# First MLP of a fused attention and two-MLP kernel: three places where weight conversions stand in the engines' queues

## The chip, the cores and the metric

The kernel runs as one launch on one core of a Trainium2 chip. The metric is the device time of the launch in microseconds (us). Engines are named as in the profile: PE does matmuls (PEld loads their weights), DVE is the vector engine, ACT the scalar engine, POOL is GpSimd, and SP issues the DMAs of this kernel. Each engine works through its own queue in order; semaphores tie the queues together.

## What is computed

Clustered attention (2 batches, 8 heads, 768 tokens, head size 64; a query sees only the keys that fall to the same of 16 centroids), then two MLPs over the 1536 tokens of 512 features. The change lies in the first MLP.

```
x = attention output, 1536 x 512
h = x @ w_in                          # 512 -> 2048
x = (h / (1 + exp(-h))) @ w_out       # 2048 -> 512
gate = 1 / (1 + exp(-(x @ w_gate)))   # second MLP, 512 -> 1536
out = (gate * (x @ w_val)) @ w_out2   # 1536 -> 512
```

The weights come as 64-bit floats and are converted on the chip; every product is made of three matmuls on a high and a low half of each operand, so that float32 accuracy is kept.

## The kernel before

**Pairs.** The hidden features of the first MLP are worked on in eight pairs of 128-wide blocks, i = 0 to 7. A pair has two layers: `hidden(i)` makes the hidden features (PE names h_0x, h_0y, h_0z, h_0w, h_0v, h_1.. in the trace all read h_0), and `mixed(i)` multiplies them with the output weights (PE name y_) and adds them into `acc`. The hidden layer is one level of a Strassen scheme (`strassen`): seven runs of 12 matmuls, x, y, z, w, X, v, W, each on one PSUM bank, whose results DVE combines (L836, L838, L855, L846, L852). ACT applies the activation (L892) and casts the high half (L64, gha); DVE, for one quarter POOL, subtracts it for the low half (L869, gla): that is `split`, and `parted` holds the last one traced. PE's order is written by hand: for i from 2 on, the runs x and y of pair i come first, then `mixed(i - 1)`, then the other runs of pair i.

**Weights.** Each pair has two input blocks (ci) and two output blocks (co), with i and e or n as numbers. One block takes these steps: SP issues a 512 KB transfer into one of two raw buffers (ri, ro; L690); ACT copies the upper words into one of three buffers (L695); POOL clips (L696); DVE does three integer steps (L701, L703, L705); then ACT casts the high half (L64) and POOL subtracts for the low half (L714) of wi.. or wo... For an input block POOL makes four sums first (L741 to L744, si). The raw buffer is free for the next transfer when L705 is done. ACT's, DVE's and POOL's queues are put in order by a scheduler; `tc.issue_after(x)` lets an instruction stand only behind x in its engine's queue.

**What sets the place of the conversions.** `weights(key)` makes the block asked for and the next two. The list `behind` holds instructions of the attention's last head, behind which the first blocks' DVE steps are put one by one: nine row maxima, and three times an entry of `copied`, the DVE copies (L67) of transposed probabilities of the last head. `copied[-2]` is the copy of rows 2 and 3 of its second half (u7_1_2), `copied[-1]` that of rows 4 and 5 (u7_1_4).

**End of the attention.** PE makes the last value products v (L501) and the row sums' reciprocals spread over partitions, rb (L580); DVE adds and scales (L513, L574, L576, L587). Then ACT (L64) and DVE (L76) split two quarters of the second batch's operand x, and DVE's L836 frees the bank that h_0v of pair 0 needs.

Of the kernel before, what the change touches and what calls it, by code (L numbers as in the profile page):

```python
# [10 lines left out]
F32 = mybir.dt.float32  # L11
# [3 lines left out]
AF = mybir.ActivationFunctionType  # L15
# [16 lines left out]
def clustered_attention_then_two_mlps(ctx, tc, qT, kT, v, cen, cenT, w1i, w1o, w2g, w2v, w2o, out):  # L32
    nc = tc.nc
    B, HP, _, S = qT.shape
# [4 lines left out]
    NT = S // P  # L39
# [4 lines left out]
    scale = 1.0 / float(D) ** 0.5  # L44
    NPAIR = B * HP
# [10 lines left out]
    ends = []  # L56
    begin = []
    maxima = []
    copied, latest, moved = [], [], []
    home = {0: xp}  # L60

    def cast(eng, o, i):
# [22 lines left out]
    def right_sums(temporary, name, b, caster, adder, kept):  # L85

        put = partial(right_operand, name, b, caster=caster, subber=adder)
        b11, b21, b12, b22 = quarters(b).values()
        t1 = temporary(f"{name}t1{b}")
        adder.tensor_tensor(t1, b12, b11, op=ALU.subtract)  # L90
        kept[b] = t1
        t2 = temporary(f"{name}t2{b}")
        adder.tensor_tensor(t2, b22, t1, op=ALU.subtract)
        put("t2", t2)
        yield
        t4 = temporary(f"{name}t4{b}")
        adder.tensor_tensor(t4, t2, b21, op=ALU.subtract)
        put("t4", t4)
        yield
        t3 = temporary(f"{name}t3{b}")  # L100
        adder.tensor_tensor(t3, b22, b12, op=ALU.subtract)
        put("t3", t3)
        yield
# [577 lines left out]

    N1, N2 = M1 // 2, M2 // 2

    behind = [maxima[(NPAIR - 1) * 2 * NT + n] for n in (4, 7, 10) for _ in range(3)] + copied[-2:-1] * 3

    def converted(src, name):

        r = rp.tile([P, KD * P], mybir.dt.int64, tag="r", name=f"r{name}")
        with tc.issue_after(loaded[0].ins):
            nc.sync.dma_start(r, src)  # L690
        words = r.bitcast(I32).rearrange("p (n w) -> p n w", w=2)
        low, up_ = words[:, :, 0], words[:, :, 1]
        t = wp.tile([P, KD * P], F32, tag="c", name=f"c{name}")
        ti = t.bitcast(I32)
        nc.scalar.activation(t, up_.bitcast(F32), AF.Copy, scale=2.0**-112)  # L695
        nc.gpsimd.tensor_scalar(t, t, LARGEST, -LARGEST, op0=ALU.min, op1=ALU.max)  # L696
        def one():
            return tc.issue_after(behind.pop(0).ins) if behind else nullcontext()

        with one():  # L700
            nc.vector.tensor_scalar(ti, ti, 3, None, op0=ALU.logical_shift_left)  # L701
        with one():
            nc.vector.scalar_tensor_tensor(ti, low, 29, ti, op0=ALU.logical_shift_right, op1=ALU.bitwise_or)  # L703
        with one():
            nc.vector.scalar_tensor_tensor(ti, up_, SIGN, ti, op0=ALU.bitwise_and, op1=ALU.bitwise_or)  # L705
        return t
# [10 lines left out]
    def plain(src, name, after=()):  # L717
        return two(converted(src, name), name, after=after)

    def four(srcs, name):  # L720

        made = {}
        for n, src in enumerate(srcs):
            pair = two(converted(src, f"{name}_{n}"), f"{name}{n}")
            for m in range(2):
                made[f"a{n + 1}{m + 1}"] = part(pair, m)
        return made
# [6 lines left out]
    def seven(srcs, name, all_four=False):  # L734

        a, b = (converted(src, f"{name}_{n}") for n, src in enumerate(srcs))
        a11, a12, a21, a22 = a[:, 0:Q], a[:, Q:], b[:, 0:Q], b[:, Q:]
        first = two(a, f"{name}a")
        t = wp.tile([P, 4, Q], F32, tag="s", name=f"s{name}", bufs=1)
        sub = nc.gpsimd.tensor_tensor  # L740
        sub(t[:, 0], a21, a22, op=ALU.add)  # L741
        sub(t[:, 1], t[:, 0], a11, op=ALU.subtract)
        sub(t[:, 2], a11, a21, op=ALU.subtract)
        sub(t[:, 3], a12, t[:, 1], op=ALU.subtract)  # L744
        after = latest if all_four else ()
        s12 = two(t[:, 0:2].rearrange("p a b -> p (a b)"), f"{name}s", after=after)
        s34 = two(t[:, 2:4].rearrange("p a b -> p (a b)"), f"{name}t", after=after)
        last = two(b, f"{name}b") if all_four else two(a22, f"{name}d", dp)
        made = dict(
            a11=part(first, 0),  # L750
            a12=part(first, 1),
            s1=part(s12, 0),
            s2=part(s12, 1),
            s3=part(s34, 0),
            s4=part(s34, 1),
            a22=part(last, 1 if all_four else 0),
        )
        if all_four:
            made["a21"] = part(last, 0)
        return made  # L760

    jobs, place = [], {}
# [22 lines left out]
    def weights(*key):  # L785

        n = place[key]
        for c in range(n, min(n + look[0] + 1, len(jobs))):
            if c not in made:
                with tc.issue_after((ends if c > AHEAD else begin)[0].ins):  # L790
                    made[c] = jobs[c]()
        return made[n]
# [67 lines left out]
    parted = []  # L860
# [28 lines left out]
    def hidden(i, bs, order="xyzwXvW"):  # L889
        def take(c, m, h, bs, inside):  # L890
            g = c if inside else temporary(f"g{i}_{m}{h}{bs.start}")[:, bs]
            nc.scalar.activation(g, c, AF.Silu)  # L892
            split(g, m, (h, bs), f"a{i}", nc.gpsimd if m and h else nc.vector)

        yield from strassen(weights("1i", i), f"h{i}", take, bs, order)

    def hidden_directly(i, b):
        def take(c, m, b):
            g = temporary(f"g{i}_{m}_{b}")
            nc.scalar.activation(g, c, AF.Silu)  # L900
            split(g, m, (slice(0, 2), b), f"a{i}", nc.vector)

        yield from direct(weights("1i", i), f"p{i}", take, b)

    def accumulate(z, o, first):
        if first:
            nc.scalar.activation(z, o, AF.Copy)
        else:
            nc.vector.tensor_tensor(z, o, z, op=ALU.add)  # L909

    def mixed(i, b=None):
        f = [[gs[f"a{i}", k, t] for t in "hl"] for k in range(2)]
        if b is None:
            f = [[t.rearrange("p h b s -> p (h b s)") for t in k] for k in f]
            parts = [slice(n * NB, (n + 1) * NB) for n in range(B * S // NB)]
            z = acc.rearrange("p d h b s -> p d (h b s)")
        else:
            f = [[t[:, :, b, :] for t in k] for k in f]
            parts = range(2)
            z = acc[:, :, :, b, :]  # L920
        for n, c in enumerate(parts):
            for e in range(2):
                o = bank(f"y{i}_{n}{e}{b}", third(2 * n + e, b is not None))
                wh, wl = (h.rearrange("p (d k c) -> p d k c", d=2, k=2) for h in weights("1o", i, e))
                width = NB if b is None else HS
                for d in range(2):
                    for k, (fh, fl) in enumerate(f):
                        for m, (s, t) in enumerate(((wh, fh), (wh, fl), (wl, fh))):
                            nc.tensor.matmul(  # L929
                                o[:, d, 0:width],  # L930
                                lhsT=s[:, d, k, :],
                                rhs=t[:, c],
                                start=k == 0 and m == 0,
                                stop=k == 1 and m == 2,
                            )
                accumulate(z[:, 2 * e : 2 * e + 2, c], o[:, :, 0:width], i == 0)
                yield
# [36 lines left out]
    def out_of(i):  # L974
# [22 lines left out]
        def last_products(n, t, u):  # L997
            z = oc[:, t : u + 1 : u - t]
            h = NB // 2
            for m, (a, c) in enumerate(((0, slice(0, NB)), (1, slice(0, h)), (1, slice(h, NB)))):  # L1000
                o = bank(f"z{i}_{t}_{m}", third(n + m, True))
                for k in range(2):
                    products(o, t, u, k, (a,), c)
                accumulate(z[:, a, c], o[:, a, c], False)
                store((t, u)[a], z[:, a, c], c)

        def evict(o, t, u):
            z = oc[:, t : u + 1 : u - t]
            accumulate(z, o, i == 0)
            if i == N2 - 1:  # L1010
                for a, q in enumerate((t, u)):
                    store(q, z[:, a])
# [32 lines left out]
    def run(gen):  # L1045
        for _ in gen:
            pass
# [9 lines left out]
    def sums(name, b):  # L1057
        return right_sums(temporary, name, b, ACT, DVE, kept)
# [19 lines left out]
    next(following)  # L1078
    run(front)
    run(following)  # L1080
    rest = sums("x", 1)
    next(rest)
    with tc.issue_after(parted[0].ins):
# [86 lines left out]
```

## Time and profile before

| what | us |
|---|---|
| three runs, median (lowest to highest) | 785.38 (781.26 to 786.43) |
| the profiled execution, own time | 783.95 |
| its span in the trace | 782.0 |
| PE busy in it | 766.4 |

The span runs from the first to the last instruction of the program; 1.95 us of the profiled execution's own time lie around it. The profiled execution is 1.43 us below the median of the three runs.

### The profile page before, as it was taken

The numbers are of one execution on the slowest core, as the hardware profiler recorded it, in microseconds if no ns is written. First come the engines' busy times: TensorE is split into PE (matmuls) and PEld (weight loads), VectorE is DVE, ScalarE is ACT, GpSimd is POOL, SyncE is SP. The second block draws the span as 40 slices with busy tenths as digits, with TensorE's granted clock in tenths as the row PEclk, the third lists the DMA queues.
The fourth block names the chain that finished last, engine by engine and source line by source line (L and its number), as shares of the span: only waits on it lengthen the run. The fifth ranks groups of instructions, "written<-read, shape, count | busy, mean of one in ns | idle before, by whom it ended". The sixth has DMA issues, their size and how long they took to land.

```text
span 782.0 us, 11463 instructions
## 1 busy us (share of the span) xinstructions
PE 766.4 (98%) x4314; PEld 653.0 (83%) x4314; DVE 628.7 (80%) x787; ACT 404.6 (52%) x691; POOL 396.5 (51%) x345
## 2 busy tenths in 40 slices
PE   8999999999999998999999999999999999999998
PEld 4766776676768986989989989998998989999896
DVE  6887787788797988879688678998497896979746
ACT  6777776777786663615525326546532425333120
POOL 5234223646664774646546326445664847748220
PEclk9999999999999999999999999999999999999999
DMA  7676467368131132222121211221021221122004
GB/s 209 161 183 151 119 159 185 103 149 228 39 102 56 53 108 81 81 81 81 54 81 55 79 56 54 81 66 64 34 81 54 81 82 54 54 66 69 1 0 162
DMA packets 25487, 71.60 MB, mean 92 GB/s; under 512 B 4484, under 2 KB 4952, under 8 KB 25432
## 3 DMA queue, kind: packets, MB, share of 16 engines
q1 hardware_dynamic: 24888, 70.84, 31.1%
q8 instruction: 34, 0.56, 0.3%
q14 instruction: 21, 0.17, 0.1%
q10 hardware_dynamic: 544, 0.03, 0.0%
HBM read 48.01 MB, written 3.19 MB: 65 GB/s over the span
## 4 chain that ended last, share of the span: by engine, by line
PE 82%; DVE 9%; ACT 3%; DMA 3%; issue 2%; SPq 0%; POOL 0%; ACTq 0%; DVEq 0%; POOLq 0%
PE z L988 12%; PE v L501 7%; PE s L454 7%; PE y L929 4%; PE t L493 4%; PE h_0w L813 3%; PE h_0x L813 3%; PE g_0w L813 2%; PE g_0x L813 2%; PE y_00None L929 2%; PE u L482 2%; PE v_0w L813 2%; PE v_0x L813 2%; PE r L879 2%; PE q L879 2%; PE y_01None L929 2%
## 5 line engine op out<-in xcount | busy, mean ns | idle before, releaser
L462 DVE TENSOR_REDUCE nm<-s 128x1 f32<-128x768 f32 x96 | 91.5, 954 | 16.1 <-PE s L454 15.2
L467 ACT ACTIVATE e<-s,nm 128x768 f32<-128x768 f32 x96 | 86.5, 901 | 27.6 <-DVE nm L462 26.8
L988 PE MATMUL z<-wu,ghb 128*128 128x512 f32 (+1 forms) x292 | 89.7, 389 | 0.5 <-DVE acc L909 0.5
L501 PE MATMUL v<-ph,vv 128*64 128x384 f32 x384 | 69.2, 494 | 0.3 <-DVE ph L67 0.3
L988 PEld LDWEIGHTS z<-wu,ghb 128*128 128x128 f32 x292 | 54.0, 188 | 12.6 <-issue 1.3
L493 PE MATMUL t<-ident,e 128*128 128x128 f32 x384 | 58.7, 276 | 1.2 <-ACT ph L64 0.4
L454 PE MATMUL s<-ka,qa 128*128 128x384 f32 x192 | 57.5, 380 | 2.0 <-ACT e L467 1.7
L988 PE MATMUL z<-wu,glb 128*128 128x512 f32 (+1 forms) x146 | 57.1, 391 | 0.0
L532 POOL TENSOR_TENSOR acc<-xf,rb 128x768 f32<-128x768 f32 x7 | 12.8, 1829 | 83.8 <-DMA rb<-d_rb 83.8
L501 PEld LDWEIGHTS v<-ph,vv 128*64 128x64 f32 x384 | 25.2, 136 | 30.7 <-issue 26.2
L64 ACT ACTIVATE ph<-t 128x512 f32<-128x512 f32 x68 | 40.7, 599 | 17.9 <-PE t L493 17.0
L454 PE MATMUL s<-k,q 128*128 128x384 f32 x192 | 49.6, 339 | 0.1
L493 PEld LDWEIGHTS t<-ident,e 128*128 128x128 f32 x384 | 43.8, 140 | 5.7 <-DVE ph L67 3.2
L909 DVE TENSOR_TENSOR acc<-z,acc 128x1024 f32<-128x1024 f32 (+2 forms) x32 | 36.6, 1154 | 13.6 <-PE z L988 12.9
L482 PEld LDWEIGHTS u<-ident,e 128*128 128x128 f32 x192 | 22.8, 140 | 25.0 <-issue 18.6
L67 DVE COPY ph<-u 128x512 f32<-128x512 f32 x48 | 32.8, 683 | 12.4 <-PE u L482 12.4
L482 PE MATMUL u<-ident,e 128*128 128x128 f32 x192 | 38.8, 284 | 0.0
L454 PEld LDWEIGHTS s<-k,q 128*128 128x128 f32 x192 | 34.5, 188 | 0.6 <-DMA k<-rows 0.4
L988 PEld LDWEIGHTS z<-wu,glb 128*128 128x128 f32 x146 | 27.4, 188 | 7.3 <-DVE glb L869 1.8
L714 POOL TENSOR_TENSOR wo<-co,wo 128x512 fp32r<-128x512 f32 x16 | 23.1, 1449 | 20.3 <-ACT wo L64 20.3
L929 PE MATMUL y<-gha,wo 128*128 128x384 f32 x128 | 32.8, 334 | 0.0
L454 PEld LDWEIGHTS s<-ka,qa 128*128 128x128 f32 x192 | 28.9, 190 | 4.5 <-ACT e L467 3.4
(627 smaller groups left out, 2138.4 us busy)
## 6 DMA issues: line engine op xcount, KB each, us to landing
ri<-in_w1i SPq DMA_DIRECT2D x16, 512.0 KB, 3.2
ro<-in_w1o SPq DMA_DIRECT2D x16, 512.0 KB, 3.2
ka<-kh SPq DMA_DIRECT2D x32, 192.0 KB, 4.0
rg<-in_w2g SPq DMA_DIRECT2D x12, 512.0 KB, 3.2
rv<-in_w2v SPq DMA_DIRECT2D x12, 512.0 KB, 3.2
ru<-in_w2o SPq DMA_DIRECT2D x12, 512.0 KB, 3.4
qq<-in_qT SPq DMA_DIRECT2D x8, 384.0 KB, 3.3
kk<-in_kT SPq DMA_DIRECT2D x8, 384.0 KB, 5.0
```

The costliest lines, as they stand in the source:

```text
L64: return nc.scalar.activation(o, i, AF.Copy)
L67: return nc.vector.tensor_copy(o, i)
L454: nc.tensor.matmul(s[:, g, 0:HS], lhsT=a[:, j, i * P : (i + 1) * P], rhs=c[:, j, g * HS : (g + 1) * HS], start=n == 0, stop=n == 1,)
L462: maxima.append(nc.vector.tensor_reduce(nm, s[:, :, 0:HS], axis=AX.XY, op=ALU.max, negate=True))
L467: x = nc.scalar.activation(e, s[:, :, 0:HS], AF.Exp, bias=nm, scale=1.0, accum_out=tots[p][:, n : n + 1])
L482: nc.tensor.transpose(both[:, kt - 4, i % 2, :], e[:, kt * P : (kt + 1) * P], ident)
L493: nc.tensor.transpose(t[:, kt, :], e[:, kt * P : (kt + 1) * P], ident)
L501: m = nc.tensor.matmul(o[(L, U)[kt % 2]], lhsT=vv[:, j, kt, :], rhs=ring[:, kt, g * G : (g + 1) * G], start=n < 2, stop=n >= NT - 2,)
L813: nc.tensor.matmul(o[:, b, 0:HS], lhsT=w[a][s][:, k, :], rhs=right[b, q][t][:, k, :], start=start and k == 0 and n == 0, stop=k == KQ - 1 ...
L909: nc.vector.tensor_tensor(z, o, z, op=ALU.add)
L929: nc.tensor.matmul(o[:, d, 0:width], lhsT=s[:, d, k, :], rhs=t[:, c], start=k == 0 and m == 0, stop=k == 1 and m == 2,)
L988: nc.tensor.matmul(o[:, a, c], lhsT=s[:, q * P : (q + 1) * P], rhs=r[:, c], start=k == 0 and m == 0, stop=k == 1 and m == 2, skip_group_ch ...
```

## The change

Four edits, all on the order of ACT's, DVE's and POOL's queues; PE's and SP's orders of instructions stay as they were, row by row.

1. The three DVE steps of pair 0's second output block (co0_1) are put behind `copied[-1]` instead of `copied[-2]`.
2. When the third pair's first input block comes to be made, ACT's copies of its two input blocks (ci2_0, ci2_1) are put behind the last two of ACT's copies of `mixed(0)` into `acc` (`firsts`).
3. When the third pair's output blocks (co2_0, co2_1) come to be made, their six DVE steps are put behind the last split of the second pair.
4. `weights("1o", 0, 1)` is called before the sums of the second batch's operand, so that the next two blocks are traced there.

```diff
-    copied, latest, moved = [], [], []
+    copied, latest, moved, firsts = [], [], [], []
...
-    behind = [maxima[(NPAIR - 1) * 2 * NT + n] for n in (4, 7, 10) for _ in range(3)] + copied[-2:-1] * 3
+    behind = [maxima[(NPAIR - 1) * 2 * NT + n] for n in (4, 7, 10) for _ in range(3)] + copied[-1:] * 3
+    paced = []
...
-        nc.scalar.activation(t, up_.bitcast(F32), AF.Copy, scale=2.0**-112)
+        with tc.issue_after(paced.pop(0).ins) if paced else nullcontext():
+            nc.scalar.activation(t, up_.bitcast(F32), AF.Copy, scale=2.0**-112)
...
             if c not in made:
+                if c == place["1i", 2]:
+                    paced.extend(firsts[-2:])
+                if c in (place["1o", 2, 0], place["1o", 2, 1]):
+                    behind.extend(parted * 3)
                 with tc.issue_after((ends if c > AHEAD else begin)[0].ins):
...
         if first:
-            nc.scalar.activation(z, o, AF.Copy)
+            firsts.append(nc.scalar.activation(z, o, AF.Copy))
...
     run(following)
+    weights("1o", 0, 1)
     rest = sums("x", 1)
```

In the rows below a name carries its pair, as in h1_0u2 (pair 1), and the number of its buffer. The changed kernel's lines are higher by up to seven: L836 is L842 there, L838 L844, L846 L852, L852 L858, L855 L861, L869 L875, L701 to L705 are L703 to L707, L695 is L697, L714 L716, L907 L913.

**DVE at the end of the attention**, before:

```order
L67 COPY ph_266<-u7_1_2_2846 128x2x256
L701 TENSOR_SCALAR co0_1_3066<-co0_1_3066 128x512
L703 SCALAR_TENSOR_TENSOR co0_1_3066<-ro0_1_3064,co0_1_3066 128x512
L574 TENSOR_SCALAR tot7_2610<-tot7_2610 128x2x3
L705 SCALAR_TENSOR_TENSOR co0_1_3066<-ro0_1_3064,co0_1_3066 128x512
L576 RECIPROCAL rs7_1_2925<-tot7_2610 128x6
L67 COPY ph_266<-u7_1_4_2874 128x2x256
L513 TENSOR_TENSOR xf7_2780<-v7_1_0_2893,other7_1_0_2900 64x384
L587 TENSOR_TENSOR acc_58<-xf7_2780,rb7_0_2906 128x384
```

and now:

```order
L67 COPY ph_266<-u7_1_2_2846 128x2x256
L574 TENSOR_SCALAR tot7_2610<-tot7_2610 128x2x3
L576 RECIPROCAL rs7_1_2925<-tot7_2610 128x6
L67 COPY ph_266<-u7_1_4_2874 128x2x256
L703 TENSOR_SCALAR co0_1_3066<-co0_1_3066 128x512
L513 TENSOR_TENSOR xf7_2780<-v7_1_0_2893,other7_1_0_2900 64x384
L705 SCALAR_TENSOR_TENSOR co0_1_3066<-ro0_1_3064,co0_1_3066 128x512
L707 SCALAR_TENSOR_TENSOR co0_1_3066<-ro0_1_3064,co0_1_3066 128x512
L587 TENSOR_TENSOR acc_58<-xf7_2780,rb7_0_2906 128x384
```

The three steps of co0_1 have moved from between the copies u7_1_2 and u7_1_4 to behind the second, around the addition xf7; the first L587 now stands behind them.

**DVE in the second pair's hidden layer**, before:

```order
L836 TENSOR_TENSOR h1_0u2_3385<-h1_0y_3399,h1_0u2_3385 128x768
L701 TENSOR_SCALAR co2_0_3534<-co2_0_3534 128x512
L703 SCALAR_TENSOR_TENSOR co2_0_3534<-ro2_0_3532,co2_0_3534 128x512
L838 TENSOR_TENSOR h1_0u3_3413<-h1_0z_3414,h1_0u2_3385 128x768
L705 SCALAR_TENSOR_TENSOR co2_0_3534<-ro2_0_3532,co2_0_3534 128x512
L855 TENSOR_TENSOR h1_0d_3441<-h1_0w_3428,h1_0u3_3413 128x768
L701 TENSOR_SCALAR co2_1_3545<-co2_1_3545 128x512
L703 SCALAR_TENSOR_TENSOR co2_1_3545<-ro2_1_3543,co2_1_3545 128x512
L705 SCALAR_TENSOR_TENSOR co2_1_3545<-ro2_1_3543,co2_1_3545 128x512
L846 TENSOR_TENSOR h1_0u3_3413<-h1_0u3_3413,h1_0v_3466 128x768
L869 TENSOR_TENSOR gla1_0_3463<-g1_000_3460,gha1_0_3462 128x768
L852 TENSOR_TENSOR h1_0u2_3385<-h1_0w_3428,h1_0u2_3385 128x768
```

and now:

```order
L842 TENSOR_TENSOR h1_0u2_3385<-h1_0y_3399,h1_0u2_3385 128x768
L707 SCALAR_TENSOR_TENSOR ci2_1_3509<-ri2_1_3507,ci2_1_3509 128x512
L844 TENSOR_TENSOR h1_0u3_3413<-h1_0z_3414,h1_0u2_3385 128x768
L861 TENSOR_TENSOR h1_0d_3441<-h1_0w_3428,h1_0u3_3413 128x768
L852 TENSOR_TENSOR h1_0u3_3413<-h1_0u3_3413,h1_0v_3466 128x768
L875 TENSOR_TENSOR gla1_0_3463<-g1_000_3460,gha1_0_3462 128x768
L858 TENSOR_TENSOR h1_0u2_3385<-h1_0w_3428,h1_0u2_3385 128x768
L875 TENSOR_TENSOR gla1_1_3445<-h1_0u3_3413,gha1_1_3444 128x768
L875 TENSOR_TENSOR gla1_0_3463<-h1_0u2_3385,gha1_0_3462 128x768
L703 TENSOR_SCALAR co2_0_3534<-co2_0_3534 128x512
L703 TENSOR_SCALAR co2_1_3545<-co2_1_3545 128x512
```

The six steps of co2_0 and co2_1 no longer stand ahead of h1_0v's, the splits' and h1_0w's instructions, but begin behind the last split.

**POOL in the same place**, before (L744 ends the sums for the third pair's input weights, wi2s and wi2t):

```order
L744 TENSOR_TENSOR si2_3518<-ci2_0_3501,si2_3518 128x256
L714 TENSOR_TENSOR wi2s_3523<-si2_3518,wi2s_3523 128x512
L714 TENSOR_TENSOR wo2_0_3540<-co2_0_3534,wo2_0_3540 128x512
L869 TENSOR_TENSOR gla1_1_3445<-h1_0d_3441,gha1_1_3444 128x768
L714 TENSOR_TENSOR wi2t_3526<-si2_3518,wi2t_3526 128x512
```

and now:

```order
L746 TENSOR_TENSOR si2_3518<-ci2_0_3501,si2_3518 128x256
L875 TENSOR_TENSOR gla1_1_3445<-h1_0d_3441,gha1_1_3444 128x768
L716 TENSOR_TENSOR wi2s_3523<-si2_3518,wi2s_3523 128x512
L698 TENSOR_SCALAR co2_1_3545<-co2_1_3545 128x512
L716 TENSOR_TENSOR wi2t_3526<-si2_3518,wi2t_3526 128x512
```

The low half of the split h1_0d now comes ahead of the low half of wi2s.

**ACT between the two pairs**, before (y0_.. are the products of `mixed(0)`, copied into acc):

```order
L64 ACTIVATE wo1_0_3273<-co1_0_3267 128x512
L907 ACTIVATE acc_58<-y0_110_3303 128x2x384
L695 ACTIVATE ci2_0_3501<-ri2_0_3499 128x512
L907 ACTIVATE acc_58<-y0_001_3317 128x2x384
L64 ACTIVATE wo1_1_3381<-co1_1_3375 128x512
L907 ACTIVATE acc_58<-y0_011_3331 128x2x384
L907 ACTIVATE acc_58<-y0_101_3345 128x2x384
L695 ACTIVATE ci2_1_3509<-ri2_1_3507 128x512
```

and now:

```order
L64 ACTIVATE wo1_0_3238<-co1_0_3232 128x512
L913 ACTIVATE acc_58<-y0_110_3303 128x2x384
L913 ACTIVATE acc_58<-y0_001_3317 128x2x384
L64 ACTIVATE wo1_1_3381<-co1_1_3375 128x512
L913 ACTIVATE acc_58<-y0_011_3331 128x2x384
L913 ACTIVATE acc_58<-y0_101_3345 128x2x384
L697 ACTIVATE ci2_0_3501<-ri2_0_3499 128x512
L913 ACTIVATE acc_58<-y0_111_3359 128x2x384
L697 ACTIVATE ci2_1_3509<-ri2_1_3507 128x512
L840 ACTIVATE h1_0u2_3385<-h1_0x_3384 128x768
```

The copy ci2_0 has gone from ahead of three copies into acc to behind them.

## Rows read from the trace of the kernel before

**Rows 1.** PE in time, second pair: start, length in us, instruction, [idle before <- releaser].

```profile
275.02 2.38 PE L813 MATMUL h_0x<-x,wi1a 128*128 128x384 f32 x12 [0.77 <-ACT acc L907]
...
288.20 2.36 PE L813 MATMUL h_0w<-x,wi1t 128*128 128x384 f32 x12 [0.34 <-DVE h_0d L855]
...
296.35 0.47 PE L929 MATMUL y_00None<-gha,wo 128*128 128x512 f32 x1 [1.26 <-DVE h_0u L852]
...
298.10 0.50 PE L929 MATMUL y_00None<-gha,wo 128*128 128x512 f32 x1 [0.82 <-ACT gha L64]
299.10 0.50 PE L929 MATMUL y_00None<-gla,wo 128*128 128x512 f32 x1 [0.50 <-DVE gla L869]
...
302.37 0.63 PE L929 MATMUL y_01None<-gha,wo 128*128 128x512 f32 x1
```

**Rows 2.** The chain that ended last: start, length in us.

```profile
305.52 2.72 PE y_10None L929 x12
...
318.50 2.08 PE h_0w L813 x12
```

**Rows 3.** One stretch: busy us by engine, then granted PE clock, DMA share, GB/s.

```profile
299.50:302.80 3.30, 3.30 (x10) 2.53 (x9) 3.22 (x5) 0.71 (x1) 0.00 (x0) 0.50 0.00 0
```

**Rows 4.** The same of instructions on co alone: DVE, ACT, POOL busy.

```profile
283.60:293.30 9.70, 7.97 (x6) 1.31 (x2) 2.08 (x2) 1.00 0.24 79
```

**Rows 5.** DVE in time, the combination of the second pair's run v.

```profile
293.29 0.94 DVE L846 TENSOR_TENSOR h_0u<-h_0u,h_0v 128x768 f32<-128x768 f32 x1
```

**Rows 6.** All waits of PE at the end of the attention: us, times, longest.

```profile
PE rb L580 <- DVE ph L67: 0.9, 1, 0.9
```

**Rows 7.** ACT in time, between the first pair and the second, and in the second.

```profile
273.60 0.66 ACT L695 ACTIVATE ci<-ri 128x512 f32<-128x512 f32 x1 [2.91 <-DMA ri<-in_w1i]
...
277.13 0.68 ACT L695 ACTIVATE ci<-ri 128x512 f32<-128x512 f32 x1 [0.25 <-DMA ri<-in_w1i]
...
289.06 0.85 ACT L64 ACTIVATE gha<-h_0d 128x768 fp32r<-128x768 f32 x1
```

**Rows 8.** The input blocks' instructions, 228 to 262 us: issues of ri, and their landing.

```profile
L690 SPq DMA_DIRECT2D ri<-in_w1i x2: 328/331/334, 231.5 to 238.7; - x2
...
DMA to landing us min/median/max: 3.3/3.3/3.3
```

**Rows 9.** POOL in time: a low half of pair 0, and later instructions.

```profile
239.12 2.51 POOL L714 TENSOR_TENSOR wo<-co,wo 128x512 fp32r<-128x512 f32 x2 [1.15 <-ACT wo L64]
...
282.70 0.73 POOL L741 TENSOR_TENSOR si<-ci 128x256 f32<-128x256 f32 x1
...
287.83 1.29 POOL L714 TENSOR_TENSOR wi2s<-si,wi2s 128x512 fp32r<-128x512 f32 x1
...
290.51 2.30 POOL L869 TENSOR_TENSOR gla<-h_0d,gha 128x768 fp32r<-128x768 f32 x1
...
317.17 1.73 POOL L714 TENSOR_TENSOR wi3s<-si,wi3s 128x512 fp32r<-128x512 f32 x1
```

**Rows 10.** PE in time: end of the attention, pair 0, and pair 3's look-ahead run.

```profile
235.44 0.44 PE L482 MATMUL u<-ident,e 128*128 128x128 f32 x2
...
246.81 1.32 PE L813 MATMUL h_0v<-xt,wi0b 128*128 128x384 f32 x6
...
328.74 2.24 PE L813 MATMUL h_0y<-xt,wi3s 128*128 128x384 f32 x12
```

**Rows 11.** DVE in time, the last steps of co0_1, and pair 0's run y combined.

```profile
233.23 1.92 DVE L701 TENSOR_SCALAR co<-co 128x512 int32<-128x512 int32 x1
...
237.92 0.68 DVE L705 SCALAR_TENSOR_TENSOR co<-ro,co 128x512 int32<-128x512 int32 x1
...
238.62 0.64 DVE L67 COPY ph<-u 128x512 f32<-128x512 f32 x1
...
246.20 0.55 DVE L836 TENSOR_TENSOR h_0u<-h_0y,h_0u 128x384 f32<-128x384 f32 x1
```

**Rows 12.** ACT in time, start of the first MLP.

```profile
243.33 1.23 ACT L695 ACTIVATE ci<-ri 128x512 f32<-128x512 f32 x2
```

## The prediction

> **What bounds the kernel now.** I read the page first: PE is busy for 766.4 of 782.0 us, so nothing is to be had from the other engines unless PE waits for them or loses its clock. Next I read PE in time and looked for the places where it idles. After the attention there is one cluster, in the second pair [rows 1]: 0.77 us before the first run of the pair, 0.34 before its last run, then 1.26, 0.82 and 0.50 at the start of the next product group, 3.69 together. The reader should compare the whole stretch with the work in it. It goes from the end of the products before (275.02 - 0.77 = 274.25) to the second product group at 302.37: 28.12 us. In it stand nine runs (seven of the pair, two of the next) at 2.08 and one product group at 2.72 [rows 2], 21.44 in all. So 6.68 us are lost: the 3.69 of idling; 1.65 from the clock, which had been granted at half (1.2 instead of 2.4 GHz) for 3.30 us right after these waits [rows 3]; and 1.34 in restarts and smaller stalls under the trace's gap threshold.
>
> Why PE waits there is read from DVE. In the 9.70 us from 283.6 on, DVE is busy for 7.97 with the six steps of co2_0 and co2_1 [rows 4], output weights that PE reads only one pair later. Run v had ended at 287.86 (288.20 - 0.34), but its combination L846 starts at 293.29 [rows 5], behind them. L846, L852, the activations and the splits hang on it one after the other, and PE's last three waits are for L852, for ACT's gha and for DVE's gla, in that order [rows 1].
>
> A smaller place is the end of the attention: PE waits 0.9 us there for a DVE copy [rows 6], the one that stands behind steps of co0_1.
>
> **The change part by part.** *The output blocks behind the last split (edit 3), with the input copies behind the layer's copies (edit 2).* First the front. ACT idles 2.91 us for a transfer of ri at 273.60 [rows 7], with the copies into acc that free PE's banks queued behind. These now go ahead, so the 0.77 us disappear and h1_0x starts at 274.25. Counting runs of 2.08 from there, v ends at 286.7, W at 288.8, the look-ahead runs at 290.9 and 293.0, and the product group would end at 295.7.
>
> Is everything else ready by then? I go along the queues. ACT's copy of ci2_0 comes behind three more copies into acc and ends near 276.6, POOL's clip 0.6 later, and its three DVE steps, at 0.68 alone [rows 11] and more beside POOL, near 279.2. The other input block's copy is held by its transfer until 277.13 as before [rows 7]; its steps, with one combination among them, end near 282.7. L846 runs when v ends, from 286.8 to 287.7 instead of 293.29. ACT has the longest queue: its copy of co2_0 waits for a transfer that can start at 279.2 and takes 3.3 [rows 8], so until 282.5. Eight ACT instructions of at most 0.85 [rows 7] (two raw copies, two weight casts, two activations, two gha) follow, and the first quarter's gha ends near 288.5. DVE's split and L852, 0.94 each like L846 [rows 5] and with 0.8 allowed for POOL, then end by 291.2, before 293.0; the next quarter's gha comes at 290.9 and its split by 292.6, before PE reads it at about 293.9. The cover is 1.3 to 1.8 us, and each us beyond it costs one.
>
> POOL is tighter. Six instructions from L741 on, which took from 282.70 to 287.83 before [rows 9], now begin at 282.7 too and end at 287.9. Then comes the split's low half, which the change puts ahead: 2.30, or 1.8 where DVE is quiet (an estimate from the ratio of 1.73 to 1.29). Then wi2s's low half, 1.29 to 1.73 [rows 9]: 291.0 to 291.9. PE's run y starts at 290.9 and reads that half from its fifth matmul, at 291.6. So 0 to 0.3 us are lost, and I take 0.3, since DVE isn't quiet. With no cluster of waits the half clock goes too. Sum here: 6.68 - 0.3 = 6.4 us gained.
>
> What is late next: the co2 steps run between the accumulations of the next product groups, where PE needs nothing of them for a pair. But the raw buffers of pair 3's input blocks come free only behind them, near 300, and PE asks for these weights 6.4 us sooner. Before, their last low half ended at 318.90 (317.17 + 1.73) [rows 9], and PE read it from 328.74 [rows 10]: 9.8 us of cover. Along the queues, with the durations above, it now ends near 317 and PE reads it from 322.3: 5 us stay.
>
> *The last block of pair 0 behind the last copy (edit 1).* Before, co0_1's three steps start at 233.23 and end at 238.60, and the copy u7_1_4, for which PE waits, ends at 239.26 [rows 11]. Now the copy goes as soon as PE has transposed (235.44 + 0.44 [rows 10]) and ends near 236.5, and the wait of 0.9 disappears. But the steps come later, and a transfer hangs on the last of them: SP issued it at 238.7, right behind L705, and it landed 3.3 later [rows 8], at 242.0. ACT's two copies of ci end at 244.56 [rows 12]; the casts of x, L76 and L836 follow, which ends at 246.75 [rows 11], 2.19 after them, and h_0v starts 0.06 after that [rows 10]. So the transfer had some 1.9 us of slack ahead of the second copy (0.6 long), and behind it this path binds PE. Now the first step starts at 236.5 and takes up to 1.92, as the row of that length did beside POOL; an addition of L836's shape 0.55, the second step 0.68 [rows 11]. The third starts at 239.2 beside POOL's low half, which starts at 239.12 and takes 1.25 [rows 9], and ends near 240.9. The transfer lands at 244.2, the copy ends at 244.9, L836 ends 2.19 later, and h_0v starts at 247.2: 0.4 us later than before, though PE stands ready 0.9 earlier. The bounds are a gain of 0.9 (steps done by 239, no POOL in the way) and a loss of 1.0 (each step as long as 1.92). I take the loss of 0.4, since POOL's queue is full there.
>
> The Trainium skill ("SBUF — State Buffer", section "Who interferes with whom") says that a DVE instruction with two SBUF inputs and a GpSimd one that reads SBUF lock each other out for a whole instruction, and that the order of issue decides which of them waits. The trace agrees that they hold each other up: a step of 0.68 where POOL was quiet, one of 1.92 beside it [rows 11]. By the rule as it stands the third step, issued a little ahead of POOL's low half, would not wait at all; that is the third rival.
>
> *The early call (edit 4).* It moves no row on any engine's queue, so it costs and brings nothing.
>
> **The rivals.** First, the wait moves on: POOL's low half of wi2s comes some 3 us late because DVE's combinations keep it out, PE idles 2.6 at run y, and the half clock returns for 1.65. That gives 783.95 - 6.68 + 2.6 + 1.65 + 0.4 = 781.9. For it speaks that POOL spent 2.30 on that split [rows 9], half of it beside DVE; against it that one more such hold-up adds about 0.5, not 3.
>
> Second, the change doesn't do what it says: the chain of late instructions had another cause, such as ACT's or the banks', and only the first 0.77 go. 783.2. Against it stands L846's place directly behind six steps that nobody was waiting for.
>
> Third, both places pay in full: co0_1's last step gets ahead of POOL's low half, and h_0v starts 0.9 earlier. 783.95 - 6.68 - 0.9 = 776.4. The row of 0.68 at 237.92 [rows 11] shows a step not held up; the one of 1.92 speaks against it.
>
> Fourth, slower than before: the orders of DVE, ACT and POOL now differ through three more pairs, and accumulations stand behind first steps on ci that wait for a late transfer. If the last low halves of a pair's input weights come later than the 5 us of cover, PE waits in each of the three pairs. It takes 2.1 us in each to eat up 6.4; at 3 us each with no half clock the time is 783.95 - 6.0 + 9 = 787. Against it: the cover of 5 us, and transfers of 3.3.
>
> **How the numbers follow.** Against the profiled execution the forecast is 783.95 - 6.4 + 0.4 = 777.95. That execution lies 1.43 below the median of the three runs, from which the same sum gives 779.4. I take 778.5, between them. Chances: forecast 0.50, wait moved to POOL 0.20, paid in full 0.18, no effect 0.07, slower 0.05. The range runs from 775.5 (paid in full, in an execution as far below the profiled one as 0.9) to 782.5 (the wait moved to POOL, from between the two starting points); it leaves out the last two rivals and some of the scatter of the runs, 781.26 to 786.43. About 1% of 785.38, so 7.85 us, is what a measurement of this kernel can tell from no change; below 777.5 it is faster by that. The forecast's own cases reach there in about a quarter, the third rival in two thirds: 0.25. Slower by over 1% has the fourth alone, 0.03; within 1% the rest, 0.72.
>
> **What the profile after would show.** Right: h1_0x without a wait; L846 of the second pair within 1 us of run v's end; the product group starting within 1 us of the look-ahead run y; no stretch of half clock in the first MLP; and a new gap of about 1 us ahead of h_0v in pair 0, with SP's second ri issue near 241. Wrong would be: a long wait of run y for POOL's low half (first rival), PE waits in the runs x and y of later pairs (fourth), or the old gaps still there (second). The sum as a whole is wrong if PE's time between the two product groups stays above 24 us.

## Result, and the profile after

The changed kernel takes 777.16 us (median of 6 runs, 776.41 to 778.92), the kernel before 783.95 (6 runs, 781.26 to 786.43): a ratio of 0.9914, 95% interval 0.989 to 0.9937. That is 6.8 us less, in the range and 1.3 below the forecast of 778.5. The profiled execution took 777.61, with a span of 775.9.

The page after, first lines (busy us and share of the span, then the granted clock in 40 slices):

```profile
span 775.9 us, 11466 instructions
...
PE 764.2 (98%) x4314; PEld 651.8 (84%) x4314; DVE 624.3 (80%) x787; ACT 404.4 (52%) x691; POOL 394.0 (51%) x345
...
PEclk9999999999999999999999999999999999999999
```

PE in time after, at the places of [rows 1, 10], then one pair later:

```profile
235.90 0.44 PE L482 MATMUL u<-ident,e 128*128 128x128 f32 x2
...
246.25 1.32 PE L819 MATMUL h_0v<-xt,wi0b 128*128 128x384 f32 x6 [0.20 <-DVE h_0u L842]
...
273.52 2.24 PE L819 MATMUL h_0x<-x,wi1a 128*128 128x384 f32 x12
...
292.24 0.39 PE L935 MATMUL y_00None<-gha,wo 128*128 128x512 f32 x1
...
295.00 0.39 PE L935 MATMUL y_01None<-gha,wo 128*128 128x512 f32 x1
...
324.11 0.47 PE L935 MATMUL y_00None<-gha,wo 128*128 128x512 f32 x1 [0.76 <-DVE h_0u L858]
...
325.49 0.50 PE L935 MATMUL y_00None<-gla,wo 128*128 128x512 f32 x1 [0.21 <-DVE gla L875]
```

The five waits of [rows 1] are gone. Two short ones have come up one pair later, where the trace of before shows none. Two rows of the chain that ended last give landmarks behind them, before:

```profile
361.93 2.76 PE y_00None L929 x12
...
761.81 16.59 PE z L988 x78
```

and after:

```profile
355.77 2.76 PE y_00None L935 x12
...
755.57 16.59 PE z L994 x78
```

From these the time can be followed stretch by stretch, counted from the last transposes of the attention (the row of `u`), ahead of which the change moves nothing:

| stretch on PE | before | after | difference |
|---|---|---|---|
| last transposes u to h_0v of pair 0 | 11.37 | 10.35 | -1.02 |
| h_0v to the end of the products ahead of pair 1 | 27.44 | 27.27 | -0.17 |
| from there to the second product group, y_01 | 28.12 | 21.48 | -6.64 |
| y_01 to the product group of pair 3 | 59.56 | 60.77 | +1.21 |
| on to the last product group of the second MLP | 399.88 | 399.80 | -0.08 |

The sum is -6.70. The span fell by 6.1 only, because in the execution after the transposes came 0.46 later (235.90 against 235.44; 234.67 in the second trace of the changed kernel, below) and the end behind the last group took 0.14 longer, neither of which the change touches.

One stretch after, to be compared with [rows 3] and with the 28.12 us of before (busy us by engine, then granted clock, DMA share, GB/s):

```profile
273.52:295.00 21.48, 21.48 (x121) 20.97 (x121) 14.11 (x17) 14.70 (x22) 13.92 (x14) 1.00 0.22 75
```

PE is busy for all of it at a granted clock of 1.00. The 21.48 us are the 21.44 that the prediction had counted as work.

### The profile page after: what moved, and what is told of

Its sections match the earlier page's. It is cut to its first block, busy times and chain, and to the rows that moved or that the text cites. A ratio compares the mean times of both kernels' runs of the same rounds, so it can differ in the third digit from the quotient of the medians.

```text
span 775.9 us, 11466 instructions
## 1 busy us (share of the span) xinstructions
PE 764.2 (98%) x4314; PEld 651.8 (84%) x4314; DVE 624.3 (80%) x787; ACT 404.4 (52%) x691; POOL 394.0 (51%) x345
## 4 chain that ended last, share of the span: by engine, by line
PE 84%; DVE 9%; ACT 3%; DMA 2%; issue 2%; POOL 0%; SPq 0%; ACTq 0%; DVEq 0%
PE z L994 12%; PE v L501 7%; PE s L454 7%; PE t L493 4%; PE y L935 4%; PE h_0w L819 3%; PE h_0x L819 3%; PE g_0w L819 2%; PE g_0x L819 2%; PE u L482 2%; PE v_0w L819 2%; PE v_0x L819 2%; PE r L885 2%; PE q L885 2%; PE y_20None L935 2%; PE y_11None L935 2%
## 5 line engine op out<-in xcount | busy, mean ns | idle before, releaser
L716 POOL TENSOR_TENSOR wo<-co,wo 128x512 fp32r<-128x512 f32 x16 | 23.9, 1501 | 28.4 <-ACT wo L64 28.4
```

## Experiments

All ratios are to the kernel before on the same chip (medians there 782.36, 782.62 and 783.08 us). One column of the table below comes from the traces: `u to h_0v` is the time from the last transposes to h_0v of pair 0, as in the table above.

**One part alone.** Edit 1 alone:

```diff
-    behind = [...] + copied[-2:-1] * 3
+    behind = [...] + copied[-1:] * 3
```

> Edit 1 alone: the steps of co0_1 behind the last copy, nothing else. Theory of the steps and the transfer (the trace of the changed kernel shows h_0v 0.56 us earlier although all before it ran 0.46 later there): PE gains 0.8 us ahead of h_0v, everything behind it shifts, the second pair's stall stays at 6.7, so 783.95 - 0.8 = 783.2, ratio 0.999. Rival (this edit carries the gain of the whole change): below 780. Rival (my predicted loss at h_0v): 784.4.

Edit 3 alone:

```diff
+                if c in (place["1o", 2, 0], place["1o", 2, 1]):
+                    behind.extend(parted * 3)
```

> Edit 3 alone: the six steps of co2 behind the second pair's last split. Theory that the stall is made by these six steps standing ahead of h1_0v's and h1_0w's combinations: 5.9 of the 6.68 us go, the 0.77 ahead of h1_0x stays, and about 1 us comes back at the next pair, so 779.0, ratio 0.994. Rival (the late input copies on ACT make the stall): no more than 1 us gained, 783.

**One part taken away.** The changed kernel without edit 3, and without edit 2:

```diff
-                if c in (place["1o", 2, 0], place["1o", 2, 1]):
-                    behind.extend(parted * 3)
```

> The change without edit 3. In the scheduler's order of this kernel only the steps of co2_0 still stand ahead of h1_0v's combination, those of co2_1 have gone behind a split by themselves, because the input copies are later. Theory of the six steps: three steps (2.1 to 3 us) fit into the 2.67 us that DVE idles ahead of that combination in the changed kernel, so most of the gain is there without the hold: 778 to 780. Rival (the hold is needed): 0.8 and 0.77 us gained, 782.4.

```diff
-                if c == place["1i", 2]:
-                    paced.extend(firsts[-2:])
```

> The change without edit 2. Theory: only the wait ahead of h1_0x (0.77 us, where a late transfer held ACT) comes back: 777.9, ratio to before 0.992. Rival (the input copies carry the gain): above 781.

| kernel | median us | ratio, interval | u to h_0v | waits of PE left in the second and third pair |
|---|---|---|---|---|
| edit 1 alone | 782.08 | 0.9996 (0.9984 to 1.0008) | 10.32 | all five of before |
| edit 3 alone | 779.33 | 0.9959 (0.9946 to 0.9972) | 11.34 | 1.16 ahead of pair 1 |
| without edit 3 | 777.02 | 0.9933 (0.9921 to 0.9946) | 10.35 | 1.01 and 0.41 in the third pair |
| without edit 2 | 776.86 | 0.9929 (0.9915 to 0.9942) | 10.46 | 0.87 at pair 1's run z |

With edit 1 alone the stall stays. PE in time, pair 1:

```profile
273.81 2.35 PE L815 MATMUL h_0x<-x,wi1a 128*128 128x384 f32 x12 [1.23 <-ACT acc L909]
...
286.90 2.36 PE L815 MATMUL h_0w<-x,wi1t 128*128 128x384 f32 x12 [0.21 <-DVE h_0d L857]
...
295.05 0.47 PE L931 MATMUL y_00None<-gha,wo 128*128 128x512 f32 x1 [1.23 <-DVE h_0u L854]
...
299.76 0.39 PE L931 MATMUL y_01None<-gha,wo 128*128 128x512 f32 x1
```

Two stretches of the same trace, around and behind these waits:

```profile
290.00:296.00 6.00, 4.75 (x25) 3.98 (x24) 4.90 (x4) 3.11 (x6) 5.75 (x4) 1.00 0.26 87
296.00:301.00 5.00, 3.70 (x15) 2.85 (x16) 4.07 (x6) 2.92 (x5) 0.61 (x1) 1.00 0.01 3
```

The reader should see two things. PE came to the pair a us earlier, and the first wait grew from 0.77 to 1.23: of the 1.05 us won at h_0v, 0.46 went straight back into it. The stretch to y_01 took 27.18 us (299.76 - 273.81 + 1.23), so 5.74 over the work. And the clock stayed at 1.00 here, where [rows 3] show 0.50 for 3.30 us behind the same waits.

Edits 2 and 3 turn out to be two ways to the same thing. Edit 3 holds the six steps back. Edit 2, by delaying the input copies, delays, relative to PE, the transfers that stand behind them, and with these the second output block's three steps. DVE in time without edit 3:

```profile
284.39 1.11 DVE L707 SCALAR_TENSOR_TENSOR co<-ro,co 128x512 int32<-128x512 int32 x1
285.42 0.94 DVE L850 TENSOR_TENSOR h_0u<-h_0u,h_0v 128x768 f32<-128x768 f32 x1
...
291.76 1.51 DVE L703 TENSOR_SCALAR co<-co 128x512 int32<-128x512 int32 x1
```

Only three of the six steps are left ahead of the combination of run v, and it is in time for PE. So either edit is enough to remove the stall (edit 2 was run only together with edits 1 and 4). What edit 2 has for itself is the place of ACT's input copies: the two kernels of the table with the hold and without edit 2 keep an ACT wait of about a us at pair 1 (1.16 and 0.87), those with edit 2 have none. But edit 2 gives it back one pair later. Without it the second pair's stretch is 1.16 us longer (22.64 against 21.48) and the third pair has no wait; from the transposes to the last group of the second MLP it comes to 519.61 us without edit 2 and 519.67 with it.

Three expectations were missed. Edit 3 alone gained less than expected (0.9959 against 0.994), and the us that was to come back at the next pair didn't come. Without edit 3 the kernel was faster than the 778 to 780 expected. Without edit 2 the wait stood at run z and not ahead of run x. By time, leaving out edit 2 or edit 3 can't be told from the changed kernel (0.9929 and 0.9933 against 0.9914 and 0.9926).

**The changed kernel once more**, beside the ones that follow.

> The changed kernel once more, as the measure for the three beside it on the same chip. Ratio to before 0.991 to 0.994, as before; PE waits of 0.76 and 0.21 us ahead of the third pair's products in the trace if they belong to the order and not to one execution.

Median 776.28, ratio 0.9926 (0.9913 to 0.9938). The waits of the third pair stand there again, with 0.49 and 0.21. The trace has one more wait that the first has not, 1.37 us for ACT in the second MLP, and so 520.92 us from the transposes to the last group in place of 519.67: two executions of one kernel can differ by that much.

**Holding more output blocks.** The hold of edit 3 extended to the fourth pair's blocks, and then to all later pairs:

```diff
-                if c in (place["1o", 2, 0], place["1o", 2, 1]):
+                if c in [place["1o", i, e] for i in (2, 3) for e in range(2)]:
```

> The changed kernel, with the steps of pair 3's output blocks also held behind the split of the pair before. Theory: the stall of the second pair was handed on in small to the third (0.76 and 0.21 us and their restarts, 1.2 in all, where DVE's h2_0w combination stands behind the steps of co3_1), so 1.2 us go: 776.0 on the chip of the first measurement, 0.9985 of the changed kernel. Rival (it is handed on again, to the pair after): the same time as the changed kernel, with the two waits one pair later.

```diff
+                if c in [place["1o", i, e] for i in range(2, N1) for e in range(2)]:
```

> The same hold for every pair of the first MLP from pair 2 on. Theory: no PE wait from the second pair to the second MLP, and 1.2 us less than the changed kernel. Rival (input weights come late when each pair's output blocks are put back, the cover of about 5 us used up): waits of PE in the runs x and y of later pairs, no gain or some us lost.

Held for two pairs, the kernel took 776.8 us, ratio 0.9925 (0.9913 to 0.9938). PE's third product group now comes without a wait:

```profile
320.12 2.24 PE L819 MATMUL h_0y<-xt,wi3s 128*128 128x384 f32 x12
322.19 0.39 PE L935 MATMUL y_00None<-gha,wo 128*128 128x512 f32 x1
```

So the waits of the third pair were co3's steps, which the hold moves away. From the transposes to the last group of the second MLP this trace has 518.18 us, 1.5 less than the changed kernel's 519.67; the timed runs don't show it. Held for all pairs it took 778.59, ratio 0.9952 (0.9938 to 0.9965): slower, though the intervals just touch. The waits are not in the runs x and y, where the rival had looked. The first MLP has one of 0.31 in its last pair, the second has two longer ones. PE in time there:

```profile
464.99 1.31 PE L819 MATMUL h_0w<-x,wi7t 128*128 128x384 f32 x6 [0.31 <-DVE h_0d L861]
...
533.06 0.71 PE L994 MATMUL z<-wu,ghb 128*128 128x512 f32 x2 [0.94 <-DVE g L971]
...
536.26 0.50 PE L994 MATMUL z<-wu,glb 128*128 128x512 f32 x1 [1.12 <-DVE glb L875]
```

The same stretch, held for two pairs:

```profile
440.00:540.00 100.00, 99.93 (x532) 93.85 (x531) 88.42 (x103) 52.06 (x81) 47.56 (x39) 1.00 0.20 68
```

and for all pairs:

```profile
440.00:540.00 100.00, 97.51 (x516) 90.94 (x515) 96.16 (x112) 52.28 (x80) 48.64 (x40) 1.00 0.21 73
```

DVE (the third engine of the row) is busy for 96.16 of 100 us in place of 88.42, and runs nine instructions more, six of them steps of the first MLP's last output blocks: what is held back in the first MLP falls where the second needs DVE, and PE waits for it. The hold of one pair thus goes on to the next, and holding everywhere only moves the collision to the end.

**One step later.** The last of co0_1's three steps put behind the first L587 that follows it; all else as changed:

```diff
-    behind = [...] + copied[-1:] * 3
+    behind = [...] + copied[-1:] * 2 + scaled_last[:1]
```

> The changed kernel with one exchange in DVE's order: the last step of co0_1 behind the multiplication into acc that follows it. Theory that the transfer issued after this step sets when h_0v can start, and that a step beside POOL's low half takes about 1.7 instead of 0.69: the step ends some 1.5 us later, so does the transfer, and PE waits 1.5 us more ahead of h_0v; 1.4 us slower than the changed kernel. Rival (the path from the last value product over ACT binds there): h_0v as before, no change.

Median 779.37, ratio 0.9952 (0.994 to 0.9965): slower than the changed kernel beside it (0.9926), by more than the 1.4 us expected. PE, DVE, POOL and ACT in time:

```profile
246.64 0.62 PE L822 MATMUL h_0v<-xt,wi0b 128*128 128x384 f32 x2 [1.04 <-DVE h_0u L845]
...
238.74 1.69 DVE L710 SCALAR_TENSOR_TENSOR co<-ro,co 128x512 int32<-128x512 int32 x1
...
238.62 1.27 POOL L719 TENSOR_TENSOR wo<-co,wo 128x512 fp32r<-128x512 f32 x1 [1.98 <-ACT wo L65]
...
243.73 0.66 ACT L700 ACTIVATE ci<-ri 128x512 f32<-128x512 f32 x1 [1.05 <-DMA ri<-in_w1i]
```

POOL's low half now started 0.12 us ahead of the step, and the step took 1.69. The transfer behind it came late, ACT waited 1.05 for it, and h_0v came 11.71 us behind the transposes, 1.36 later than after the change. That is the path of the prediction, in the very form that it forecast, one DVE instruction away from the changed kernel.

**The changed kernel without edit 1**, and the two-pair hold without edit 2:

```diff
-    behind = [...] + copied[-1:] * 3
+    behind = [...] + copied[-2:-1] * 3
```

> The changed kernel without edit 1 (co0_1's three DVE steps stand behind the copy of rows 2 and 3 again), edits 2 and 3 kept. Theory (edits 2 and 3 pay in full, and edit 1 brings about 1 us at h_0v by itself): the wait of rb for the DVE copy returns with 0.9 us, h_0v starts some 11.1 us behind the first transposes' h_0x run instead of 9.6 to 9.7, the second pair's stretch stays at about 21.5 us, and the ratio to the kernel before is 0.994 (0.9926 and 0.9914 with edit 1, plus 1 us of 783). Rival A (what edit 1 brings at h_0v is lost again behind it, since alone it timed 0.9996): the same gaps, but a ratio of 0.9926 or below. Rival B (my forecast: edit 1 costs 0.4): ratio 0.992 or below and h_0v earlier than in the changed kernel.

Median 777.85, ratio 0.9934 (0.9919 to 0.995). The wait of [rows 6] is back, and h_0v is 11.44 us behind the transposes (245.86 against 234.42):

```profile
238.38 0.93 PE L580 MATMUL rb<-ident,rs 128*64 128x128 f32 x10 [0.94 <-DVE ph L67]
...
245.86 1.33 PE L819 MATMUL h_0v<-xt,wi0b 128*128 128x384 f32 x6
```

The gaps are those that the theory expects, and so is the ratio; but its interval takes in 0.9926 as well, so the timing alone doesn't tell a us from nothing.

> Edit 1, and the six output steps held behind the last split in two pairs (third and fourth), with the input copies left where they were (no edit 2). Theory (the hold alone takes DVE's steps out of the way in the second pair, holding them one pair longer takes away the 0.7 us at the third pair, and what is left without edit 2 is one ACT wait of 0.9): no wait in the third pair's product group, a wait of 0.8 to 0.9 at h1_0z, ratio 0.992 to 0.993. Rival (edit 2 matters once the third pair is clean too, because the late input copies push the held steps into the fourth pair): waits of more than 1 us in the fourth or fifth pair and a ratio above 0.994.

Median 776.34, ratio 0.9913 (0.9899 to 0.9927). PE waits 0.50 for ACT ahead of pair 1, where 0.8 to 0.9 was expected at run z, and nowhere else in the pairs; the rival's waits in later pairs don't come. This kernel, the two-pair hold with edit 2 and the changed kernel can't be told apart by time (0.9913, 0.9925, and 0.9914 and 0.9926): no version beat the changed one measurably.

## Why the prediction was right, point by point

**The bound and its cause: right.** The stall in the second pair was DVE's six steps on co2. Four kernels that move all or half of them away lose it (edit 3 alone, edits 1 and 2, edits 1 and 3, the change itself); edit 1 alone keeps it. So the second rival, no effect, is out.

**Edits 2 and 3, 6.4 us: right, 0.2 too small.** The whole difference to the counted work came back, 6.64. The subtracted 0.3 didn't come. POOL and DVE in time after:

```profile
285.75 1.86 POOL L875 TENSOR_TENSOR gla<-h_0d,gha 128x768 fp32r<-128x768 f32 x1
287.57 1.30 POOL L716 TENSOR_TENSOR wi2s<-si,wi2s 128x512 fp32r<-128x512 f32 x1
...
286.20 0.95 DVE L852 TENSOR_TENSOR h_0u<-h_0u,h_0v 128x768 f32<-128x768 f32 x1 [2.67 <-PE h_0v L819]
```

The combination of run v starts 0.20 us behind v's end (286.20 against 286.00), and not 5.43 behind as in [rows 5] (293.29 against 287.86). POOL's low half of wi2s ended at 288.87, where I had 291.0 to 291.9, for a PE that came to the pair 0.73 later. PE's run y reads it from 290.9, so the first rival, the wait moved to POOL, had about 2 us of room and was far off. My 1.8 for the split's low half should have been 1.7 by the ratio that it names; it took 1.86, which changes nothing here.

**Edit 1, a loss of 0.4: wrong, a gain of 1.0.** This is the step that failed, and the third rival had it right. In the eight traces with edit 1 as written the time from u to h_0v is 10.19 to 10.46, and in the three without it 11.34 to 11.44. DVE and POOL in time at that place, after:

```profile
236.37 0.69 DVE L67 COPY ph<-u 128x512 f32<-128x512 f32 x1 [1.00 <-PE u L482]
...
238.50 0.71 DVE L705 SCALAR_TENSOR_TENSOR co<-ro,co 128x512 int32<-128x512 int32 x1
239.25 0.69 DVE L707 SCALAR_TENSOR_TENSOR co<-ro,co 128x512 int32<-128x512 int32 x1
...
239.57 2.75 POOL L716 TENSOR_TENSOR wo<-co,wo 128x512 fp32r<-128x512 f32 x2 [1.98 <-ACT wo L64]
```

I had the third step start at 239.2, 0.08 behind POOL's low half (239.12), and end at 240.9. In the trace after, everything at this place runs 0.46 later, so its 239.25 for the step is 0.4 earlier than I had it, while its 239.57 for POOL is just what I had. The term with the wrong size is the first step: a third step at 239.2 leaves it some 1.5 (236.5, then the addition's 0.55 and the second step's 0.68), and it took 0.90. So the third step started 0.32 ahead of POOL, took 0.69 and ended at 239.94. It was POOL that gave way: its two low halves took 2.75, against 2.51 in [rows 9]. Counted from u, the transfer was issued 1.3 us earlier than I had it (at 240.02), ACT waited 0.19 for it, and PE 0.20 at h_0v.

The path that I had named is real (a step beside POOL gives the late transfer, as the run with the step one place later shows); I chose the wrong side of a margin of 0.4 us. It was not the luck of one execution: in all eight traces with edit 1 as written the step starts 0.32 to 0.36 ahead of POOL and takes 0.69. The Trainium skill ("SBUF — State Buffer", section "Who interferes with whom") says that the order of issue decides which of the two blocks. The two traces agree: 0.69 with the step 0.32 ahead, 1.69 with it 0.12 behind. The two rows of [rows 11] that the prediction set side by side for this are not of a kind: the row of 1.92 is a first step (TENSOR_SCALAR), that of 0.68 a third (SCALAR_TENSOR_TENSOR).

**The fourth rival: it came, small.** The prediction looked for lateness in pair 3's input weights, with 5 us of cover, and these were in time. It did not follow the chain one link further. SP's issues of these input blocks wait until the held co2 steps are done; in time, before:

```profile
287.35 6.40 SPq L690 DMA_DIRECT2D ri<-in_w1i  x2
302.61 5.59 SPq L690 DMA_DIRECT2D ro<-in_w1o  x2
```

and after:

```profile
298.39 0.92 SPq L691 DMA_DIRECT2D ri<-in_w1i  x2
306.93 3.69 SPq L691 DMA_DIRECT2D ro<-in_w1o  x2
```

The first of the ro transfers, which carry pair 3's output blocks, is 4.3 us later though PE is 7 us earlier. So their six steps, which before lay between accumulations, now fall where co2's had lain, among the third pair's combinations and splits. DVE in time after:

```profile
315.76 1.68 DVE L707 SCALAR_TENSOR_TENSOR co<-ro,co 128x512 int32<-128x512 int32 x1
317.36 0.94 DVE L852 TENSOR_TENSOR h_0u<-h_0u,h_0v 128x768 f32<-128x768 f32 x1
318.23 1.20 DVE L703 TENSOR_SCALAR co<-co 128x512 int32<-128x512 int32 x1
319.47 1.67 DVE L705 SCALAR_TENSOR_TENSOR co<-ro,co 128x512 int32<-128x512 int32 x1
321.05 2.05 DVE L875 TENSOR_TENSOR gla<-g,gha 128x768 fp32r<-128x768 f32 x1
323.02 0.94 DVE L858 TENSOR_TENSOR h_0u<-h_0w,h_0u 128x768 f32<-128x768 f32 x1
```

Two steps (2.9 us together) stand between the combinations of v and w (L852 and L858), ahead of a split that took 2.05, and PE waits 0.76 for L858. It costs 1.21 in this one pair and ends there.

The hold alone does not make this wait, though. SP, DVE and PE in time without edit 2:

```profile
303.98 4.99 SPq L691 DMA_DIRECT2D ro<-in_w1o  x2
...
316.72 1.67 DVE L707 SCALAR_TENSOR_TENSOR co<-ro,co 128x512 int32<-128x512 int32 x1
318.31 0.94 DVE L850 TENSOR_TENSOR h_0u<-h_0u,h_0v 128x768 f32<-128x768 f32 x1
...
320.84 0.94 DVE L856 TENSOR_TENSOR h_0u<-h_0w,h_0u 128x768 f32<-128x768 f32 x1
...
323.12 0.39 PE L933 MATMUL y_00None<-gha,wo 128*128 128x512 f32 x1
```

Here the first ro transfer comes 9.05 us behind y_01 (294.93), after the change 11.93. The last of the six steps ends ahead of run v's combination, w's follows 2.53 later in place of 5.66, and PE doesn't wait. In all five traces with edit 2 and no second hold PE waits in the third pair, 0.7 to 1.4 us together (one of them, without edit 3, has no hold at all), and in the five without edit 2 it doesn't. So it takes the late input copies of edit 2 to make the next pair late for PE; by which step they do so was not followed. The prediction had priced this at nothing. In place of 6.4 - 0.4 = 6.0 the sum is 6.64 + 0.17 + 1.02 - 1.21 + 0.08 = 6.70: two misses of over a us that nearly cancel, which is luck.

**The half clock: charged in full, paid in part.** The forecast gained 1.65 us from it. Yet the run with edit 1 alone has 3.99 us of waits at the same places (1.23, 0.21, 1.23, 0.83, 0.49) and no stretch of half clock. So of the 6.64, a part that differs from execution to execution hangs on the clock. The record has the mean granted clock of most executions. It is 0.997 in the traced one of before, which holds the 3.30 us at 0.50. Of 36 others of that kernel, 16 have 0.997 or 0.998 and 20 have 0.999 or 1.0, and in the three measurements the medians of the first group lie 0.9 to 1.8 us above those of the second. All 11 of the changed kernel have 0.999 or 1.0. By these means the kernel before lost clock in somewhat under half of its executions, where the forecast charged the loss to all; at which place the executions without a trace lost it is not on record.

**Edit 4** was not run by itself, so that it moves no row on any engine is not shown by a run.

## What to carry to other kernels

Work that is prepared far ahead belongs behind the last instruction of the stage that somebody waits for, but each hold also holds the buffer, the next transfer and the next block's work: follow that chain until the cover is used up, and hold for as few stages as pay (here one or two; all of them cost 2 us). A copy that is put back can do the same: edit 2 saved 1.16 us in one pair and cost 1.21 in the next, which only the run without it shows. A gain ahead of a stall can go in part into the next wait: of the 1.05 us that edit 1 alone won, 0.46 went that way, and its time (0.9996) doesn't show the rest. Where two instructions may collide within some tenths of a us, give both outcomes their price, since one DVE instruction's place decided 1.4 us at h_0v here.

## What was not expected of the hardware

The same waits of PE, 3.7 and 4.0 us in all, were followed by 3.30 us at a granted clock of 0.50 in one execution and by none in another. And the hold-up between DVE and POOL is not even: a step that started 0.32 us ahead of POOL's instruction took its 0.69, and POOL's instruction beside it 1.51 where the next one took 1.28, while one that started 0.12 behind took 1.69, a us more, and ended 0.54 after POOL's instruction (240.43 against 239.89).
